# Attention over a long cache: transfers of 64 KiB a partition from one shared memory, 101 units kept between the layers, deviation applied to the products

## The chip, the core and the metric

The kernel runs on one core of one Trainium2 chip. The metric is the device time of one execution in microseconds, lower is better. A core has engines that run side by side: PE multiplies matrices (PEld loads their weights), DVE, ACT and POOL work on vectors, and SP issues the transfers from the chip's memory (HBM). The transfers themselves are carried out by 16 DMA engines, which fetch rows for the 128 partitions of the core's own memory.

## What is computed

Four blocks run one after the other on two tokens: attention, a gated feedforward, and both again with the same weights and the same cache. Each has a layernorm ahead and a residual sum behind it. The cut reference:

```python
def _A_ref(x, k_cache, v_cache, wq, wo):        # x: (2, 1, 512); caches: (2, 8, 32768, 128)
    q = (x @ wq).reshape(B, Sq, 32, 128).transpose(0, 2, 1, 3)
    k = jnp.repeat(k_cache, 4, axis=1)
    v = jnp.repeat(v_cache, 4, axis=1)
    p = _softmax(jnp.einsum("bhqd,bhkd->bhqk", q, k) * 128 ** -0.5, axis=-1)
    o = jnp.einsum("bhqk,bhkd->bhqd", p, v)
    return o.transpose(0, 2, 1, 3).reshape(B, Sq, 4096) @ wo
def _B_ref(x, w_gate, w_up, w_down):            # 512 -> 1792 -> 512
    h = _gelu(x @ w_gate) * (x @ w_up)
    return h @ w_down
for layer in range(2):
    x = x + _A_ref(_layernorm(x), A_k_cache, A_v_cache, A_wq, A_wo)
    x = x + _B_ref(_layernorm(x), B_w_gate, B_w_up, B_w_down)
```

All of it is in float32. K and V together are 512 MiB, read once in each layer. The weights are 8 MiB of wq, 8 MiB of wo, 7 MiB of gate and up (gu) and 3.5 MiB of down (wd), read in each layer too.

## The kernel before

**A layer** takes the 16 pairs of a K/V head and a batch row (`orders`, the second layer in reverse). For each pair `scores` (L226) multiplies the queries with K, `softmax` (L231 to L255) makes the probabilities and turns them, `values` (L269) multiplies them with V, `combine` (L279 to L286) picks the four heads, and after each second pair `project` (L291) multiplies with 1 MiB of wo and adds up in the PSUM tile W. Then `residual` (L296 to L304), `layernorm` (L178 to L192) and `feedforward` (L314 to L337) follow. `layernorm` and `queries` (L203 to L215) open the layer.

**The memory** for what is fetched is 12 slots of 2 MiB (16 KiB in each partition), each of two halves. K and V come in transfers of one whole slot: 128 rows of 16 KiB, 8 of K and 8 of V for a pair. Weights come in halves of 1 MiB with rows of 8 KiB (gu: 7 KiB). The units that this text counts in are 256 KiB: what one matrix multiplication reads (128 partitions x 512 numbers). A slot holds 8 of them.

**The order of transfers** is one list, `stream`. `pump` walks down it and issues each on SP (L92) as soon as a slot or a half is free. `done` gives a slot back and pumps. SP works in order, so the first transfer that has to wait holds back all behind it. Eight completion semaphores are used in turn; a ninth transfer waits until the one eight places ahead of it has landed.

**Between the layers** one slot of K (`KEEPK`) and eight of V (`KEEP`) of the last pair stay where they are, since the second layer begins with that pair. That is 72 units. The three other slots carry the rest of the last pair, then gu, wd and wq, in halves of 1 MiB.

## Time and profile before

| what | value |
|---|---|
| time, median of 3 runs | 2631.04 us (2629.43 to 2633.91) |
| span of the profiled execution | 2629.7 us |
| instructions | 20472 |
| DMA packets of the queue that SP issues on | 80928, 1110.48 MB |
| TensorE clock granted, mean | 0.778 |
| PE busy, DVE busy, ACT busy | 59%, 6%, 2% |

The page gives the span of the profiled execution from its first to its last instruction; the times of the runs are taken around it. A row of the timeline reads: start in us, duration in us, engine, line, operation, what it writes and reads, how many instructions were merged into the row, and in brackets how long the engine had been idle before and what ended that. A product in float32 stands as two MATMUL instructions, so "x8" in a row of 128x512 is four units.

### The profile page before, as it was taken

To read this page: it belongs to the slowest core of one execution; us is meant where nothing else is said; L and a number is where in the kernel's file an instruction comes from. 1 tells how busy PE (TensorE), PEld (TensorE's weight loads), DVE (VectorE), ACT (ScalarE), POOL (GpSimd) and SP (SyncE) were. 2 spreads that over 40 slices of the span, in tenths; PEclk is the share of its full clock that TensorE was granted. 3 is DMA by queue.
4 is the path that set the end of the run, shared out by engine and by line. 5 is a ranking of instruction groups with operands and counts; after the bars stand their busy time and mean duration, and the time that the engine had idled before them with its cause. 6 is when DMAs were issued, how large, how long until landed. Compare 5 with 4: busy or idle time off the path is not lost.

```text
span 2629.7 us, 20472 instructions
## 1 busy us (share of the span) xinstructions
...
## 2 busy tenths in 40 slices
...
DMA  9999999999999999999999999999999999999997
GB/s 411 428 428 427 428 427 428 428 427 427 428 428 427 429 427 428 428 428 428 407 380 415 428 427 429 427 429 427 428 428 428 427 428 428 428 427 428 428 428 332
DMA packets 81303, 1111.99 MB, mean 423 GB/s; under 512 B 9280, under 2 KB 9408, under 8 KB 11712
## 3 DMA queue, kind: packets, MB, share of 16 engines
q1 hardware_dynamic: 80928, 1110.48, 99.5%
...
q14 instruction: 14, 0.11, 0.0%
HBM read 1110.64 MB, written 0.00 MB: 422 GB/s over the span
## 4 chain that ended last, share of the span: by engine, by line
DMA 93%; PE 5%; DVE 1%; issue 0%; ACT 0%; SPq 0%; POOLq 0%; POOL 0%; DVEq 0%; ACTq 0%
DMA slot<-in_vt 49%; DMA slot<-in_kt 42%; PE S L226 2%; PE A L269 1%; DMA slot<-in_wq 1%; PE S L314 1%; PE W L337 0%; DVE mx L231 0%; DMA slot<-in_gu 0%; PE T L248 0%; ACT big L245 0%; PE small L203 0%; DMA xT<-in_x 0%; PE small L282 0%; PE W L291 0%
## 5 line engine op out<-in xcount | busy, mean ns | idle before, releaser
L226 PE MATMUL S<-slot,qpad 128*32 128x512 f32 x4096 | 674.8, 793 | 474.3 <-DMA slot<-in_kt 472.8
L269 PE MATMUL A<-slot,pT 128*16 128x512 f32 x4096 | 683.1, 809 | 429.9 <-DMA slot<-in_vt 429.9
L226 PEld LDWEIGHTS S<-slot,qpad 128*32 128x32 f32 x4096 | 132.4, 129 | 994.2 <-DMA slot<-in_kt 644.2
L269 PEld LDWEIGHTS A<-slot,pT 128*16 128x16 f32 x4096 | 117.0, 113 | 948.3 <-DMA slot<-in_vt 552.6
L231 DVE TENSOR_REDUCE mx<-S 128x1 f32<-128x512 f32 x64 | 44.2, 691 | 1141.3 <-PE S L226 1141.3
L248 PE MATMUL T<-cst,big 128*128 128x128 f32 x256 | 61.1, 384 | 68.4 <-ACT big L245 40.4
L279 DVE TENSOR_SCALAR big<-A,linv 128x512 f32<-128x512 f32 x32 | 24.0, 751 | 1090.0 <-PE A L269 1090.0
L245 ACT ACTIVATE big<-S,bias 128x512 f32<-128x512 f32 x64 | 43.4, 683 | 2449.5 <-DVE bias L241 2449.5
L248 PEld LDWEIGHTS T<-cst,big 128*128 128x128 f32 x256 | 39.2, 190 | 84.4 <-ACT big L245 65.7
L249 DVE COPY pT<-T 128x512 f32<-128x512 f32 x64 | 44.2, 691 | 97.8 <-PE T L248 97.8
L282 PE MATMUL small<-cst,big 128*128 128x128 f32 x128 | 26.1, 337 | 29.9 <-DVE big L279 29.9
L238 PE MATMUL small<-cst,nm 128*128 128x128 f32 x32 | 11.3, 354 | 34.3 <-DVE nm L236 34.3
L203 PE MATMUL small<-slot,xpad 128*32 128x512 f32 x128 | 22.4, 822 | 13.7 <-DMA slot<-in_wq 10.7
L282 PEld LDWEIGHTS small<-cst,big 128*128 128x128 f32 x128 | 16.7, 167 | 78.0 <-DVE big L279 78.0
L291 PE MATMUL W<-slot,oT 128*2 128x512 f32 x128 | 23.4, 814 | 5.1 <-DVE oT L286 5.1
L314 PE MATMUL S<-slot,xpad 128*32 128x256 f32 x224 | 19.6, 483 | 5.2 <-DVE xpad L192 2.9
L251 PEld LDWEIGHTS small<-ls,cst 128*128 128x128 f32 x64 | 17.3, 331 | 0.0
L238 PEld LDWEIGHTS small<-cst,nm 128*128 128x128 f32 x32 | 4.6, 144 | 76.5 <-DVE nm L236 70.8
L251 PE MATMUL small<-ls,cst 128*128 128x2 f32 x64 | 13.5, 280 | 0.0
L245 ACT ACTIVATION_READ_ACCUMULATOR big<-S,bias 128x1 f32 x64 | 12.5, 196 | 0.0
L337 PE MATMUL W<-slot,pT 128*2 128x512 f32 x56 | 11.1, 897 | 1.0 <-DVE pT L331 1.0
L314 PEld LDWEIGHTS S<-slot,xpad 128*32 128x32 f32 x224 | 9.4, 135 | 14.6 <-issue 5.8
...
## 6 DMA issues: line engine op xcount, KB each, us to landing
slot<-in_kt SPq DMA_DIRECT2D x255, 2048.0 KB, 39.1
slot<-in_vt SPq DMA_DIRECT2D x246, 2048.0 KB, 39.1
...
```

What stands on the lines that cost most here:

```text
L203: nc.tensor.matmul(qp[32 * t:32 * t + 32, :], window(k, v), w[:, t, :], start=(k == 0 and v == 0), stop=(k == KC - 1 and v == 1))
L226: nc.tensor.matmul(S[32 * t:32 * t + 32, u, :], qpad[:, g, b, 28 - 4 * c:60 - 4 * c], w[:, 4 * cc + t, :], start=(c == 0), stop=(c == 7))
L231: nc.vector.tensor_reduce(mx[:, u:u + 1], S[:, u, :], axis=AX.X, op=OP.max)
L245: nc.scalar.activation(p[u], S[:, u, :], AF.Exp, bias=bias, scale=SCALE, accum_out=ls[:, u:u + 1])
L248: nc.tensor.transpose(T[:, u, k * P:(k + 1) * P], p[u][:, k * P:(k + 1) * P], ident)
L249: nc.vector.tensor_copy(pT[:, u].rearrange("p k r -> p (k r)"), T[:, u, :])
L251: nc.tensor.matmul(m[:, :2], same, ls, start=True, stop=True)
L269: nc.tensor.matmul(A[32 * t:32 * t + 16, :], pT[:, u, k, 32 * t + 16 * e:32 * t + 16 * e + 16], we[:, t, :], start=(n == 0 and e == 0), st ...
L279: nc.vector.tensor_scalar(md, A, linv, None, op0=OP.mult)
L282: nc.tensor.transpose(m[:, c * P:(c + 1) * P], md[:, c * P:(c + 1) * P], ident)
L291: nc.tensor.matmul(W[32 * t:32 * t + NB, :], oT[:, t, :], w[:, t, :], start=first, stop=final)
L314: nc.tensor.matmul(S[32 * t:32 * t + 32, which, :FN], window(k, v), w[:, r, :], start=(k == 0 and v == 0), stop=(k == KC - 1 and r + 4 >= FR))
```

## The change

K and V are fetched in transfers of 8 MiB, 128 rows of 64 KiB each, 32 units. All of the slots become one tile M of 110 units: three slots A, B and C of 32 units that are used in turn, and three places of four units (`PL`; the last two units of the third are also the buffers of the probabilities). Every transfer has its place in M written down in `plan`. A pair now has 4 transfers of K and V, and the first wq comes in two of 4 MiB.

Between the layers 101 units of the last pair stay: all 64 of V in A and B, the second half of K (32) in C, and five units of the first half of K, which ACT and DVE copy into five PSUM banks. The weights and what is missing of K pass through the three places in transfers of 1 MiB. The second layer first multiplies the kept half of K, four units after each four of wq, and the pieces of the other half of K take the units that come free.

The layernorm is taken apart. `center` subtracts the mean with matrix products; `deviation` works out the reciprocal deviation while the next products already run, and the products are multiplied by it (`scaled`, and the first instructions of the gelu). In `feedforward` gate and up of one block lie side by side, and the 28 units are worked through in two parts of 16 and 12, each followed by its own gelu. `combine` picks the heads with products too, and divides afterwards. In the second layer the last chunk of V comes in pieces of 24, 4 and 4 units (as in the first), gu in four and wd in five transfers into the slots, and the last four units of wd are used as weights of the products, so that the sum comes out turned.

```diff
-NT = 8
-COLS = 4096
-HALF = COLS // 2
+SEQ = 32768
+U = 512
+CH = 32
...
-SLOTS = 12
-KEEP = 8
-KEEPK = 1
+NU = 110
+SLOT_A, SLOT_B, SLOT_C, ZONE = 0, 32, 64, 96
+PL = [96, 100, 104]
+U_P0, U_P1, U_PT = 106, 107, 108
+NPS = 5
+KFREE = CH - NPS
...
-    slots = [cp.tile([P, COLS], F32, name=f"slot{i}") for i in range(SLOTS)]
-    free = [(i, h) for i in range(SLOTS) for h in range(2)]
...
+    M = cp.tile([P, NU * U], F32, name="M")
...
+    def mem(u, n=1):
+        return M[:, u * U:(u + n) * U]
...
     def pump():
-        while stream:
-            key, src, shape = stream[0]
-            n = int(np.prod(shape[1:]))
-            spot = take(n > HALF)
-            if spot is None:
+        while plan:
+            key, src, u, n = plan[0]
+            if any(busy[u:u + n]):
                 return
-            stream.popleft()
-            i, h = spot[0]
-            at[key] = spot, slots[i][:shape[0], h * HALF:h * HALF + n]
-            nc.sync.dma_start(at[key][1], src)
+            plan.popleft()
+            for i in range(u, u + n):
+                busy[i] = True
+            live[key] = u
+            nc.sync.dma_start(mem(u, n), src)
...
+    def free(u, n=1):
+        for i in range(u, u + n):
+            assert busy[i], i
+            busy[i] = False
         pump()
...
+    def chunk(name, l, g, b, h, base, cuts=(CH,), turn=0):
+        src = (kt if name == "k" else vt)[b, g, h]
+        lo = 0
+        where = {}
+        for n in cuts:
+            u = base + (lo + turn) % CH
+            add((name, l, g, b, h, lo), cols(src, lo, n), u, n)
+            for i in range(n):
+                where[lo + i] = ((name, l, g, b, h, lo), u + i)
+            lo += n
+        pieces[(name, l, g, b, h)] = where
...
+        if l == 0:
+            stream("wq", 0, wq, 32, (16, 16), (SLOT_A, SLOT_A + 16))
+            ring = [SLOT_B, SLOT_C, SLOT_A]
+            todo = [(g, b, nm_, h) for g, b in orders[0] for nm_ in "kv" for h in range(2)]
+        else:
+            ring = [SLOT_A, SLOT_B, SLOT_C]
+            g, b = orders[1][0]
+            add(("wq7",), cols(wq, 28, 4), PL[1], 4)
+            stream("wq", 1, wq, 28, (4,) * 7, [PL[0], PL[2], PL[1], PL[0], PL[2], PL[1], PL[0]])
+            where = {}
+            lo = 0
+            for n, u in [(4, PL[2])] + [(4, SLOT_C + 4 * i) for i in range(5)] + [(KFREE - 24, PL[0])]:
+                key = ("k", 1, g, b, 0, lo)
+                add(key, cols(kt[b, g, 0], lo, n), u, n)
+                for i in range(n):
+                    where[lo + i] = (key, u + i)
+                lo += n
+            pieces[("k", 1, g, b, 0)] = where
+            g, b = orders[1][1]
+            chunk("k", 1, g, b, 0, SLOT_C, (12, 20), 20)
+            chunk("k", 1, g, b, 1, SLOT_A, (16, 16))
+            chunk("v", 1, g, b, 0, SLOT_B)
+            add(("wo", 1, g), wo[g], wo_place(g), 4)
+            chunk("v", 1, g, b, 1, SLOT_C)
+            todo = [(g, b, nm_, h) for g, b in orders[1][2:] for nm_ in "kv" for h in range(2)]
+        for i, (g, b, nm_, h) in enumerate(todo):
+            last = i == len(todo) - 1
+            second = (g, b) == orders[l][orders[l].index((g, b))] and orders[l].index((g, b)) % 2 == 1
+            if nm_ == "v" and h == 1 and second and not (last and l == 0):
+                add(("wo", l, g), wo[g], wo_place(g), 4)
+            chunk(nm_, l, g, b, h, ring[i % 3], (24, 4, 4) if last else (CH,))
+            if last and l == 0:
+                add(("wo", l, g), wo[g], wo_place(g), 4)
+        if l == 0:
+            stream("gu", 0, gu, 28, (4,) * 7, [PL[0], PL[2], PL[1], PL[0], PL[2], PL[1], PL[0]])
+            stream("wd", 0, wd, 14, (4, 4, 4, 2), [PL[2], PL[1], PL[0], PL[2]])
+        else:
+            stream("gu", 1, gu, 28, (8, 8, 8, 4), [SLOT_C + 8 * i for i in range(4)])
+            stream("wd", 1, wd, 14, (8, 2, 2, 1, 1), [SLOT_A, SLOT_A + 8, SLOT_A + 10, SLOT_A + 12, SLOT_A + 13])
...
+    def halves(dst, src):
+        nc.scalar.copy(dst[:, :U // 2], src[:, :U // 2])
+        nc.vector.tensor_copy(dst[:, U // 2:], src[:, U // 2:])
+    def center():
+        ws = mem(U_PT + 1)
+        nc.scalar.activation(ws[:, :U // 2], W[:, :U // 2], AF.Copy, accum_out=rs[:, 0:1])
+        nc.vector.tensor_tensor_reduce(ws[:, U // 2:], W[:, U // 2:], zero, 1.0, 0.0, OP.add, OP.add, rs[:, 1:2])
+        for c in (2, 3, 0, 1):
+            nc.tensor.matmul(X[:, c * 4:(c + 1) * 4], ws[:, c * P:(c + 1) * P], two, start=(c == 2), stop=False)
+        for j in range(2):
+            nc.tensor.matmul(X[:, :KC * 4], rs[:, j:j + 1].to_broadcast([P, P]), neg, start=False, stop=(j == 1))
+        xc = X[:, :KC * 4].rearrange("p (c w b) -> p c w b", w=2, b=NB)
+        nc.vector.tensor_copy(xw[:, :, XO:XO + NB], xc[:, :, 1, :])
+        nc.scalar.copy(xin, xc[:, :, 0, :])
+        for b in range(NB):
+            xb = xw[:, :, XO + b]
+            nc.vector.tensor_tensor_reduce(junk, xb, xb, 1.0, 0.0, OP.mult, OP.add, sq2[:, b:b + 1])
+    def deviation(B):
+        v = B[:, 32:32 + NB]
+        nc.tensor.matmul(v, ones.to_broadcast([P, P]), sq2, start=True, stop=True)
+        nc.vector.tensor_tensor_reduce(junk[:, :NB], v, par, 1.0, EPS, OP.mult, OP.add, var)
         nc.gpsimd.tensor_tensor(rstd, var, half, op=OP.pow)
...
+    def scaled(dst, src):
+        nc.scalar.activation(dst[:, :U // 2], src[:, :U // 2], AF.Copy, scale=rstd)
+        nc.vector.tensor_scalar(dst[:, U // 2:], src[:, U // 2:], rstd, None, op0=OP.mult)
...
+    def combine(acc, oT, b):
+        md = mem(U_PT)
+        halves(md, acc)
+        for c in (2, 3, 0, 1):
+            nc.tensor.matmul(X[:, :REP], md[:, c * P:(c + 1) * P], sel[:, 4 * c:4 * c + 4],
+                             start=(c == 2), stop=(c == 1))
+        nc.vector.tensor_tensor(oT[:, :, b], X[:, :REP], linv, op=OP.mult)
...
+        center()
+        s = 0
+        G = [bank[5], bank[7]]
+        g, u, a, th = [mem(U_PT + j // 2)[:, (j % 2) * FN:(j % 2 + 1) * FN] for j in range(4)]
+        for v in range(2):
+            nt = 4 if v == 0 else 3
+            for k in range(KC):
+                for t in range(nt):
+                    key, un = where[s]
+                    at(key)
+                    nc.tensor.matmul(G[v][32 * t:32 * t + 32, :], xw[:, k, XO:XO + 32], mem(un),
+                                     start=(k == 0), stop=(k == KC - 1))
+                    if cut[key] == s:
+                        for q in range(28):
+                            if where[q][0] == key:
+                                free(where[q][1])
+                    s += 1
+                if v == 0 and k == 0:
+                    deviation(X)
...
+            nc.scalar.activation(a[:R], gp, AF.Square, scale=r)
+            nc.vector.tensor_scalar(g[:R], gp, r, None, op0=OP.mult)
+            nc.scalar.activation(u[:R], up, AF.Copy, scale=r)
+            nc.vector.tensor_scalar(a[:R], a[:R], 0.044715, 1.0, op0=OP.mult, op1=OP.add)
+            nc.vector.tensor_tensor(a[:R], a[:R], g[:R], op=OP.mult)
+            nc.vector.tensor_tensor(u[:R], u[:R], g[:R], op=OP.mult)
+            nc.scalar.activation(a[:R], a[:R], AF.Tanh, scale=math.sqrt(2.0 / math.pi))
+            nc.vector.tensor_scalar(a[:R], a[:R], 0.5, 0.5, op0=OP.mult, op1=OP.add)
+            nc.vector.tensor_tensor(th[:R], a[:R], u[:R], op=OP.mult)
+            for j in range(2):
+                nc.tensor.matmul(G[v][:, j * 8:(j + 1) * 8], th[:, j * P:(j + 1) * P], selt, start=True, stop=True)
...
+        tail = 4 if l == 1 else 0
+        for n in range(FD - tail):
+            key, un = where[n]
+            at(key)
+            r, j = divmod(n, 2)
+            v, t = divmod(r, 4)
+            nc.tensor.matmul(W[32 * (n % 4):32 * (n % 4) + NB, :], hT[:, v, j, 2 * t:2 * t + NB], mem(un),
+                             start=(0 < n < 4), stop=(n + 4 >= FD - tail))
+            free(un)
+        if tail:
+            ws = mem(U_PT + 1)
+            halves(ws, W)
+            for c in (2, 3, 0, 1):
+                nc.tensor.matmul(X[:, c * NB:(c + 1) * NB], ws[:, c * P:(c + 1) * P], sel[:, :NB],
+                                 start=(c == 2), stop=False)
+            for n in range(FD - tail, FD):
+                key, un = where[n]
+                at(key)
+                r, j = divmod(n, 2)
+                v, t = divmod(r, 4)
+                for c in range(KC):
+                    nc.tensor.matmul(X[:, c * NB:(c + 1) * NB], mem(un)[:, c * P:(c + 1) * P],
+                                     hT[:, v, j, 2 * t:2 * t + NB], start=False,
+                                     stop=(n == FD - 1 and c == KC - 1))
+            y = sm[:, 0:8]
+            nc.vector.tensor_copy(y, X[:, :KC * NB])
+            nc.sync.dma_start(out, y)
...
+        if (g, b) == last:
+            k0 = pieces[("k", 0, g, b, 0)]
+            free(k0[0][1], KFREE)
+            for i in range(KFREE, KFREE + 3):
+                (nc.scalar.copy if i % 2 else nc.vector.tensor_copy)(bank[psum[i]], mem(k0[i][1]))
+                free(k0[i][1])
+            def hold(h):
+                i = KFREE + 3 + h
+                nc.scalar.copy(bank[psum[i]], mem(k0[i][1]))
+                free(k0[i][1])
+                if h == 1:
+                    free(PL[2], 4)
+            softmax(S, hold)
...
+    center()
+    g, b = last
+    u = at(("wq7",))
+    Q7 = bank[5]
+    for k in range(KC):
+        query_unit(Q7, 7, k, u + k, True, True)
+    free(u, 4)
+    deviation(X)
...
+    for gg in range(7):
         for k in range(KC):
+            key, u = where[4 * gg + k]
+            at(key)
+            query_unit(X, gg, k, u, gg == 0, gg == 6)
+        free(where[4 * gg][1], 4)
+        n = 4 if gg < 6 else CH - i
+        for j in range(n):
+            score_unit(S1, w, i, k1[i][1], i < 4, i >= CH - 4)
+            free(k1[i][1])
...
+    where = pieces[("k", 1, g, b, 0)]
+    held = {30: PL[1], 31: PL[1] + 1, 27: PL[1] + 2, 28: PL[1] + 3, 29: PL[0] + 3}
+    seq = list(range(24)) + [30, 31, 27, 28, 29] + [24, 25, 26]
...
+    values(1, g, b, A1, [pieces[("v", 0, g, b, h)] for h in range(2)], False, 16)
+    combine(A1, oTs[1], b)
...
-        "kt": f(kc.reshape(NB, HKV, NT, COLS, P).transpose(0, 1, 2, 4, 3)),
-        "vt": f(vc.reshape(NB, HKV, 2, 2, 2, 2, 4, 4, P, P).transpose(0, 1, 2, 7, 8, 3, 6, 4, 5, 9)
-                ).reshape(NB, HKV, NT, P, COLS),
+        "kt": f(kc.reshape(NB, HKV, 2, SEQ // 2, P).transpose(0, 1, 2, 4, 3)),
+        "vt": f(vc.reshape(NB, HKV, 2, 2, 4, 4, 4, P, P).transpose(0, 1, 2, 7, 6, 3, 5, 4, 8)
+                ).reshape(NB, HKV, 2, P, CH * U),
```

SP's order shows the sizes. This is the start of the second pair of a layer in the kernel before, which issues K and V of the pair into slots of 2 MiB (4096 numbers a row); the names are tile and tensor:

```order
L92 DMA slot_74<-in_kt 128x4096
L92 DMA slot_75<-in_kt 128x4096
L92 DMA slot_76<-in_kt 128x4096
L92 DMA slot_77<-in_kt 128x4096
L92 DMA slot_66<-in_kt 128x4096
```

In the changed kernel the same place on SP reads as follows; the waits are those written into the instruction, on completion semaphores of transfers (DMAHW) and on PE:

```order
L110 DMA M<-in_kt 128x16384 [waits DMAHW5_49,DMAHW0_49,PE_49]
L110 DMA M<-in_kt 128x16384 [waits DMAHW6_49,PE_49]
L110 DMA M<-in_vt 128x16384 [waits DMAHW7_49,DMAHW2_49,PE_49]
L110 DMA M<-in_wo 128x2048
L110 DMA M<-in_vt 128x16384 [waits DMAHW0_49,PE_49]
```

One row now stands for what were four, and each waits for PE's last reading of its slot. The next place is the end of the first layer. Before, SP issues there the last half of V, then gu, wd and wq:

```order
L92 DMA slot_68<-in_wo 128x2048 [waits DMAHW0_49,PE_49]
L92 DMA slot_68<-in_vt 128x2048 [waits DMAHW1_49,PE_49]
L92 DMA slot_70<-in_vt 128x2048 [waits DMAHW2_49,PE_49]
L92 DMA slot_70<-in_gu 128x1792 [waits DMAHW3_49,PE_49]
L92 DMA slot_71<-in_gu 128x1792 [waits DMAHW4_49,PE_49]
L92 DMA slot_71<-in_gu 128x1792 [waits DMAHW5_49,PE_49]
```

Now the same place on SP is:

```order
L110 DMA M<-in_vt 128x12288 [waits DMAHW7_49,PE_49]
L110 DMA M<-in_vt 128x2048 [waits PE_49,Activation_49]
L110 DMA M<-in_vt 128x2048 [waits Activation_49]
L110 DMA M<-in_wo 128x2048
L110 DMA M<-in_gu 128x2048
L110 DMA M<-in_gu 128x2048 [waits PE_49]
L110 DMA M<-in_gu 128x2048 [waits DMAHW5_49,DMAHW0_49,PE_49]
```

wo has moved behind V, two transfers of gu follow it into free places, and the third of gu waits for PE's reading of wo. The last place is PE's feedforward in the second layer. Before (the name S is the PSUM tile of gate and up, small and W are PSUM, pT is the turned gelu):

```order
L314 MATMUL S<-slot_70,xpad 32x256 [waits DMAHW6_49]
L314 MATMUL S<-slot_70,xpad 32x256 x6
L330 MATMUL small<-cst,big 128x128 [waits DVE_49,PE_49]
L330 MATMUL small<-cst,big 128x128
L337 MATMUL W<-slot_70,pT 2x512 [waits DMAHW7_49,DVE_49]
L337 MATMUL W<-slot_70,pT 2x512 x3
```

And in the changed kernel (bank_79 and bank_81 are the PSUM banks of the two parts, bank_80 is W):

```order
L367 MATMUL bank_79<-M,xw 32x512 x7
L391 MATMUL bank_79<-cst,M 128x8 [waits DVE_49,Activation_49]
L391 MATMUL bank_79<-cst,M 128x8
L367 MATMUL bank_81<-M,xw 32x512 [waits DMAHW2_49]
L367 MATMUL bank_81<-M,xw 32x512 x7
L367 MATMUL bank_81<-M,xw 32x512 [waits DMAHW3_49]
L367 MATMUL bank_81<-M,xw 32x512 x3
L391 MATMUL bank_81<-cst,M 128x8 [waits DVE_49,Activation_49,Pool_49]
L391 MATMUL bank_81<-cst,M 128x8
L401 MATMUL bank_80<-M,hT 2x512 [waits DMAHW4_49]
```

The products of the first gelu (L391) stand on PE between the two parts of gu, so PE waits there for ACT and DVE a first time before it can go on with the second part, and a second time behind it.

501 lines of the change are left out of this document (247 added, 254 removed).

## Prediction

> **What bounds the kernel now.** The page comes first: the span, the DMA slices, the chain, and how long one transfer takes to land.
>
> ```profile
> span 2629.7 us, 20472 instructions
> DMA  9999999999999999999999999999999999999997
> GB/s 411 428 428 427 428 427 428 428 427 427 428 428 427 429 427 428 428 428 428 407 380 415 428 427 429 427 429 427 428 428 428 427 428 428 428 427 428 428 428 332
> q1 hardware_dynamic: 80928, 1110.48, 99.5%
> DMA 93%; PE 5%; DVE 1%; issue 0%; ACT 0%; SPq 0%; POOLq 0%; POOL 0%; DVEq 0%; ACTq 0%
> slot<-in_kt SPq DMA_DIRECT2D x255, 2048.0 KB, 39.1
> slot<-in_vt SPq DMA_DIRECT2D x246, 2048.0 KB, 39.1
> ```
>
> The transfers set the time: 93% of the chain is DMA, and the rate is flat at 428 GB/s outside three places (start, slices 20 to 22, end). So three things can change it: fewer bytes, a higher flat rate, and the places where the queue runs dry. At 428 GB/s a transfer of 2 MiB takes 2.097/0.428 = 4.90 us; eight in flight need 39.1 us to land, 4.89 each.
>
> A transfer with rows half as long has its own row. At the start PE waits for each 1 MiB of wq (8 KiB rows):
>
> ```profile
> 16.33 1.06 PE L203 MATMUL small<-slot,xpad 128*32 128x512 f32 x8 [1.42 <-DMA slot<-in_wq]
> ...
> 23.79 1.94 PE L203 MATMUL small<-slot,xpad 128*32 128x512 f32 x8 [1.42 <-DMA slot<-in_wq]
> ```
>
> Three periods lie between: 7.46/3 = 2.487 us for 1 MiB. Two of them take 4.974, against 4.89 to 4.90 for the same bytes in one transfer. So there is a fixed part of 0.074 to 0.084 us in each transfer, whatever its bytes; I take **0.08**. It may belong to the transfer or to its 8 rows for each DMA engine; both counts are the same here.
>
> **The change, part by part.**
>
> *Bytes.* 72 units are kept now and 101 then: 29 units, 7.25 MiB, 3.63 transfers of 2 MiB at 4.90 us: **-17.8 us**.
>
> *Fixed parts.* The issues count 561 now (255 of K, 246 + 4 of V, 16 each of wq, wo and gu, 8 of wd), and 183 in the changed program (137 of K and V, 10 of wq, 16 of wo, 11 of gu, 9 of wd). 378 fewer at 0.08 us: **-30.2 us** (bounds: 0, if a row of 64 KiB is cut up on its way; 378 x 0.084 = 31.8). An 8 MiB transfer then takes 4 x 4.895 - 3 x 0.08 = 19.34 us, or 434 GB/s. I take nearly the upper end, since the fixed part is seen between two sizes of this very kernel.
>
> The Trainium skill, "DMA: Bandwidth & Descriptors", Rules for kernel authors, holds 1 MiB a transfer for enough; by it the term would be 0. The rows already differ: 2.487 against 2.45 us per MiB above 1 MiB.
>
> *Cover for the large transfers.* PE may give a slot back only after a whole chunk of 32 units. How fast PE works stands here:
>
> ```profile
> 1400.69 16.43 PE L269 MATMUL A<-slot,pT 128*16 128x512 f32 x128
> 2586.59 3.48 PE L269 MATMUL A<-slot,pT 128*16 128x512 f32 x16 [2.98 <-DMA slot<-in_vt]
> 2591.56 1.05 PE L269 MATMUL A<-slot,pT 128*16 128x512 f32 x8 [1.49 <-DMA slot<-in_vt]
> 2594.04 1.91 PE L269 MATMUL A<-slot,pT 128*16 128x512 f32 x8 [1.43 <-DMA slot<-in_vt]
> ```
>
> 64 units take 16.43 us; 8 units after a wait 3.48, so PE is slow first. A chunk is then 3.5 + 24 x 0.23 = 9.0 us. Behind it two more slots are being filled, 38.7 us. The cover holds three times over: 0 us.
>
> *Between the layers.* The five-microsecond windows of before, where the queue falls short (last column GB/s; the one before, the DMA share):
>
> ```profile
> 1305.00:1310.00 5.00, 3.75 (x20) 0.82 (x12) 0.97 (x2) 0.00 (x0) 0.00 (x0) 0.50 0.73 305
> 1310.00:1315.00 5.00, 1.54 (x12) 1.02 (x8) 1.93 (x9) 0.00 (x0) 0.69 (x1) 0.84 0.76 297
> 1315.00:1320.00 5.00, 4.82 (x44) 2.26 (x47) 0.13 (x1) 0.00 (x0) 0.00 (x0) 0.50 0.43 125
> 1320.00:1325.00 5.00, 4.00 (x62) 2.00 (x54) 0.00 (x0) 0.00 (x0) 0.00 (x0) 0.96 0.98 325
> 1355.00:1360.00 5.00, 3.35 (x19) 0.62 (x12) 0.94 (x3) 0.00 (x0) 0.00 (x0) 0.70 0.77 270
> 1360.00:1365.00 5.00, 3.64 (x32) 0.94 (x32) 0.04 (x1) 0.00 (x0) 0.00 (x0) 1.00 0.92 380
> 1400.00:1405.00 5.00, 5.00 (x29) 1.58 (x31) 0.92 (x3) 0.00 (x0) 0.00 (x0) 0.50 0.82 351
> 1405.00:1410.00 5.00, 5.00 (x48) 1.18 (x44) 0.00 (x0) 0.00 (x0) 0.00 (x0) 0.92 0.96 341
> ```
>
> What is missing to 428, times 5 us, over 428, adds up to 12.0 us lost. For the changed kernel I walk along the list, from the landing of the last piece of V, with steps from the feedforward at the end of the program, which runs the same code:
>
> ```profile
> 2596.07 0.75 DVE L279 TENSOR_SCALAR big<-A,linv 128x512 f32<-128x512 f32 x1 [33.89 <-PE A L269]
> ...
> 2600.34 0.69 DVE L296 COPY big<-W 128x512 f32<-128x512 f32 x1 [2.08 <-PE W L291]
> ...
> 2602.29 0.30 PEld L178 LDWEIGHTS small<-xn,avg 128*128 128x128 f32 x2 [0.79 <-PE small L299]
> ...
> 2605.29 9.75 PE L314 MATMUL S<-slot,xpad 128*32 128x256 f32 x112 [1.50 <-DVE xpad L192]
> ...
> 2615.10 0.38 ACT L319 ACTIVATE big<-S 128x256 f32<-128x256 f32 x1 [56.37 <-PE S L314]
> ...
> 2619.08 6.19 PE L337 MATMUL W<-slot,pT 128*2 128x512 f32 x28 [0.52 <-DVE pT L331]
> ...
> 2625.33 0.69 DVE L296 COPY big<-W 128x512 f32<-128x512 f32 x1 [6.30 <-PE W L337]
> ...
> 2627.19 0.35 SPq L358 DMA_DIRECT2D out<-xn  x1
> ```
>
> Behind V three transfers lie in the queue (wo and two of gu): 7.5 us. The 24-unit piece lands 5.0 us ahead of the last, and 32 units take 9.0, so PE ends at 4.0. Combine and project take 4.3 (2596.07 to 2600.34), which frees wo's place at 8.3; data flow about 1.3 later, as these rows show, in which PE ends with wq at 1358.2 and the DMA share is back behind 1359:
>
> ```profile
> 1356.42 1.82 PE L203 MATMUL small<-slot,xpad 128*32 128x512 f32 x8 [0.55 <-DMA slot<-in_wq]
> ...
> 1358.00:1359.00 1.00, 0.24 (x4) 0.00 (x0) 0.68 (x1) 0.00 (x0) 0.00 (x0) 1.00 0.04 16
> 1359.00:1360.00 1.00, 0.66 (x4) 0.42 (x4) 0.25 (x3) 0.00 (x0) 0.00 (x0) 1.00 1.31 279
> ```
>
> Gap 9.6 - 7.5 = 2.1. The next place comes free after centering (4.95 now from 2600.34 to 2605.29, some 1.5 less without the variance) and four units of gu: about 12.8, data at 14.1, while the one transfer in between ends at 12.1: gap 2.0. From there the three places hold 7.5 us of transfers, more than a gelu (2615.10 to 2619.08: 4.0 us), so the two gelus are covered. Behind wd the second centering gives one more gap of about 2, the turn from the queries to K another. The sum is 8 us against 12: **-4 us** (bounds -8, if the gaps close, to +8, if each gap is twice as long).
>
> *The end.* From the last V (2594.04) to the program's last transfer (2627.19) stand 33.2 us. The 42 units of gu and wd need 25.7 us of it, so PE's chain is what ends last, and I go through it: V ends at +4.0 instead of +2.0; combine and project alike; centering -1.5; gu 9.75 alike; one more gelu on PE's path, +4.0; then 8.1 us from wd to the end (2619.08 to 2627.19) become 10 units (4.4 at the slow rate of the 3.48 row), two half copies (1.0), 20 products with weights of 128x128 in two passes, 0.15 us a pass in the row at 2602.29, twice that when PE is slow (6.0 to 12.0; I take 6.5) and a copy, 12.2: +4.1. Sum +8.6; as parts may overlap I take **+7 us** (bounds 0 to +13). Where the cover of the transfers is longer than thought, this is less.
>
> *Start, copies to PSUM, softmax.* They lie beside 19.3 us of transfer each: 0.
>
> The sum: -17.8 - 30.2 - 4 + 7 = -45. On the profiled execution 2629.7 - 45 = 2584.7; the median lies 1.3 above that span, so **2586 us**.
>
> **The rivals.**
>
> *A, rows are cut up.* The change doesn't do what it says to the rate: a row of 64 KiB travels as four of 16, so the fixed part stays. Then only the 10 fewer transfers of weights count, 0.8 us of the 30.2: 2586 + 29 = 2615. For it: 80928 packets are 562 x 144, with the transfer of the result: one packet for each of 128 rows and 16 more, and no row over 16 KiB is seen. The packet count of after decides.
>
> *B, three places are too few.* 22 transfers pass through them, some 7 rounds. If a round costs 4 us more (a gelu uncovered each time): 2614. Against it: 7.5 us of transfer against 4.0 of gelu.
>
> *C, slower.* The engines walk down rows that begin 64 KiB apart instead of 16, and if such starts collide in the memory the flat rate falls. It decides from 45/124.8 = 0.36 us more for each of the 124.8 times 8 MiB, 19.70 us or 426 GB/s; at the lowest rate that the rows show for a full queue, the 2.487 us of wq (421.6 GB/s, 19.90 us), it is 0.56 x 124.8 = +70: 2656. Against it: transfers of 1 MiB show the same period with rows next to each other (wo and the first half of V, 2586.59 to 2591.56: 4.97 for two) and with rows 16 KiB apart (wq, 2.487).
>
> The Trainium skill, "DMA: Bandwidth & Descriptors", Latency and other measured facts, has rates that fall where rows lie a large power of two apart: 207 of 214 GB/s at 512 KiB, half at 4 MiB. By that 3% the time would be an estimated 2586 + 124.8 x 19.34 x 0.034 = 2668; no run here shows 64 KiB.
>
> **How the numbers follow.** My forecast 0.67 (2571 to 2601, from the bounds of the gaps and the end); A 0.13; B 0.07; C 0.11; no change at all 0.02. Within 0.2% (5 us), about what a measurement of this kernel can tell from no change, lies only the last. Faster 0.87, same 0.02, slower 0.11. The range takes in A and B and leaves out C: 2571 to 2622.
>
> **What would show it.** Right: packets of the queue near 184 x 144 = 26,500; flat slices at 433 or 434; landings of K and V 19.3 us apart; three or four gaps of 2 us behind the first layer; some 40 us from the last V to the end, with two gelus. A has 80,000 packets or slices at 428. B has a dip deeper than 380 in the middle slices. C has slices under 426. Wrong would also be a PE that makes SP wait for a slot in mid-layer.

## The result, and the profile after

| kernel | median us (lowest to highest, runs) | to the kernel before, 95% interval |
|---|---|---|
| before | 2630.99 (2629.43 to 2633.91, 4) | 1 |
| changed | 2604.99 (2602.04 to 2608.30, 4) | 0.9907 (0.9892 to 0.9922) |

Faster by 26.0 us; the forecast was 45 us faster, 2586. The time is inside the stated range (2571 to 2622), but 4 us above the part of it that belongs to the forecast's own mechanism (2571 to 2601): it is inside because the range takes in the rivals A and B. Of all the forecasts B's 2614 lies nearest. The profiled execution of the changed kernel is the fastest of its four runs (2602.04 us, span 2599.9).

The page of the changed kernel, the lines that answer to those of before:

```profile
span 2599.9 us, 20241 instructions
GB/s 421 434 433 434 432 434 429 433 435 434 430 433 431 429 435 435 431 433 434 367 352 440 431 433 430 434 434 433 434 431 431 432 430 434 434 433 434 431 428 272
q1 hardware_dynamic: 26496, 1102.86, 98.5%
DMA 58%; PE 28%; another core or an unknown queue 12%; DVE 1%; issue 1%; ACT 1%; SPq 0%; POOL 0%; ACTq 0%; DVEq 0%; POOLq 0%
```

26,496 packets are exactly 184 x 144: a row of 64 KiB is one packet. The flat slices stand at 429 to 435 instead of 427 to 429. The chain gives PE 28%; a likely reason is that with one transfer per chunk PE starts when 8 MiB have landed and SP waits for PE to give the slot back, so that the chain is followed through PE. That isn't a bound: a chunk takes PE half of the period. TensorE's rows that begin with a landing, in the middle of the first layer (the bracket holds the idle time and what ended it):

```profile
359.68 8.66 PE L286 MATMUL bank<-M,qw 128*32 128x512 f32 x64 [5.59 <-DMA M<-in_kt]
379.05 9.21 PE L286 MATMUL bank<-M,qw 128*32 128x512 f32 x64 [10.72 <-DMA M<-in_kt]
398.50 9.71 PE L330 MATMUL bank<-M 128*16 128x512 f32 x64 [5.91 <-DMA M<-in_vt]
417.85 2.76 PE L330 MATMUL bank<-M 128*16 128x512 f32 x12 [9.63 <-DMA M<-in_vt]
```

They start 19.4 us apart (58.17/3 = 19.39), at a landing each, and the forecast had 19.34. SP does wait for PE in mid-layer, which the prediction names as a sign of being wrong: the waits of SP for PE's reading of V, and the median time of 60 transfers of K from issue to landing, are these.

```profile
SPq L110 <- PE bank L330: 561.5, 62, 12.9
...
M<-in_kt SPq DMA_DIRECT2D x60, 50.4
```

But 50.4 us are two and a half periods, so other transfers lie in the queue meanwhile, and the landings keep their distance: the sign came, and it cost nothing. So the dip between the layers (367 and 352 GB/s) and the one at the end (272) must hold what is missing. The first is the sign that the prediction gave for rival B, a dip deeper than 380.

The window of the changed kernel over the whole stretch behind the first layer, and the five-microsecond windows in it that move least (the clock is the third column from the end, GB/s the last):

```profile
1285.00:1355.00 70.00, 51.39 (x328) 17.86 (x321) 9.59 (x39) 6.87 (x18) 1.41 (x3) 0.80 0.80 307
...
1285.00:1290.00 5.00, 5.00 (x48) 1.18 (x40) 0.00 (x0) 0.00 (x0) 0.00 (x0) 1.00 0.61 247
1290.00:1295.00 5.00, 2.68 (x24) 1.61 (x20) 1.02 (x4) 0.85 (x3) 0.00 (x0) 0.98 0.39 126
1295.00:1300.00 5.00, 4.74 (x24) 2.76 (x27) 0.68 (x7) 0.17 (x1) 0.04 (x1) 0.50 0.47 188
1310.00:1315.00 5.00, 4.08 (x24) 0.90 (x18) 0.35 (x1) 0.47 (x1) 0.00 (x0) 0.82 0.46 149
1335.00:1340.00 5.00, 5.00 (x29) 1.23 (x33) 0.34 (x2) 0.00 (x0) 0.00 (x0) 0.59 0.41 133
```

What is missing to 434 is (434 - 307)/434 of 70 us, 20.5 us; the forecast was 8, and before lost 12. (These transfers of 1 MiB have rows of 8 KiB, which took 2.487 us a MiB in the kernel before, 422 GB/s; against that it is 19.1 us.) How it comes about, in the changed kernel's timeline of all engines (SPq is SP's queue of issues, L110 the line that issues every transfer):

```profile
1293.46 12.05 SPq L110 DMA_DIRECT2D M<-in_gu  x5
...
1295.95 1.01 PE L244 MATMUL bank<-cst,sm 128*128 128x16 f32 x4
...
1297.22 1.94 PE L367 MATMUL bank<-M,xw 128*32 128x512 f32 x8 [0.26 <-DVE xw L246]
...
1304.06 1.06 PE L367 MATMUL bank<-M,xw 128*32 128x512 f32 x8 [1.57 <-DMA M<-in_gu]
...
1305.27 0.47 ACT L381 ACTIVATE M<-bank,sm 128x256 f32<-128x256 f32 x1 [7.91 <-PE bank L367]
...
1309.12 4.96 PE L367 MATMUL bank<-M,xw 128*32 128x512 f32 x24
```

And the view of line 110 between 1290 and 1310 us, how long those five transfers of 1 MiB took from issue to landing:

```profile
DMA to landing us min/median/max: 4.7/4.9/6.5
```

The first two, each issued into an empty queue, needed 4.7 and 4.8 us, of which 2.5 are the transfer. The walk had put 1.3 on it instead of 2.3. And PE gives no place back while it waits for the gelu (1305.27 to 1309.12) or works through centering. So a place is out for 4.7 us or more after it was freed, and the other two hold 5 us of stream at best. The rows of the end, from the landing of the 24-unit piece of the last V:

```profile
2550.92 8.71 PE L330 MATMUL bank<-M 128*16 128x512 f32 x64 [8.34 <-DMA M<-in_vt]
...
2576.58 3.63 PE L367 MATMUL bank<-M,xw 128*32 128x512 f32 x24
...
2584.67 4.43 PE L401 MATMUL bank<-M,hT 128*2 128x512 f32 x17
...
2591.02 6.25 PE L416 MATMUL bank<-hT,M 128*128 128x2 f32 x32
...
2597.54 0.35 SPq L421 DMA_DIRECT2D out<-sm  x1
```

The last V lands about 5.0 us behind the first row (two transfers of 1 MiB at 2.49), at 2555.9; from there to the last transfer stand 41.6 us, 8.4 more than before's 33.2. (The expectations below count to the end of the span, 44.2.)

### The profile page after: what moved, and what is told of

The parts are those of the page before. It is cut to its first block, busy times and chain, and to the rows that moved or that the text cites. A ratio compares the mean times of both kernels' runs of the same rounds, so it can differ in the third digit from the quotient of the medians.

```text
span 2599.9 us, 20241 instructions
## 1 busy us (share of the span) xinstructions
PE 1370.0 (53%) x9456; PEld 409.2 (16%) x9456; DVE 147.2 (6%) x433; ACT 73.1 (3%) x196; POOL 3.2 (0%) x12
## 3 DMA queue, kind: packets, MB, share of 16 engines
q1 hardware_dynamic: 26496, 1102.86, 98.5%
## 4 chain that ended last, share of the span: by engine, by line
DMA 58%; PE 28%; another core or an unknown queue 12%; DVE 1%; issue 1%; ACT 1%; SPq 0%; POOL 0%; ACTq 0%; DVEq 0%; POOLq 0%
DMA M<-in_vt 50%; PE bank L330 16%; PE bank L286 8%; DMA M<-in_kt 6%; DMA cst<-in_consts 1%; PE bank L348 1%; PE bank L341 1%; PE bank L367 1%; PE bank L259 1%; DVE M L235 0%; PE bank L401 0%; ACT M L234 0%; PE bank L416 0%; PE bank L242 0%
## 5 line engine op out<-in xcount | busy, mean ns | idle before, releaser
L286 PE MATMUL bank<-M,qw 128*32 128x512 f32 x4096 | 582.3, 731 | 534.8 <-DMA M<-in_kt 534.8
L330 PE MATMUL bank<-M 128*16 128x512 f32 x4096 | 580.1, 730 | 530.9 <-DMA M<-in_vt 530.9
L286 PEld LDWEIGHTS bank<-M,qw 128*32 128x32 f32 x4096 | 142.2, 131 | 963.7 <-DMA M<-in_kt 575.3
L330 PEld LDWEIGHTS bank<-M 128*16 128x16 f32 x4096 | 137.2, 112 | 947.2 <-issue 947.1
L289 DVE TENSOR_REDUCE sm<-bank 128x1 f32<-128x512 f32 x64 | 44.3, 692 | 1107.1 <-PE bank L286 1107.1
L311 ACT ACTIVATE M<-bank,sm 128x512 f32<-128x512 f32 x64 | 43.4, 682 | 1229.3 <-DVE sm L306 1229.3
L314 PE MATMUL bank<-cst,M 128*128 128x128 f32 x256 | 49.2, 335 | 40.6 <-ACT M L311 40.3
L315 DVE COPY M<-bank 128x512 f32<-128x512 f32 x64 | 43.8, 692 | 60.7 <-PE bank L314 60.7
L234 ACT COPY M<-bank 128x256 f32<-128x256 f32 x33 | 12.3, 372 | 1162.0 <-PE bank L330 1155.2
L314 PEld LDWEIGHTS bank<-cst,M 128*128 128x128 f32 x256 | 34.9, 169 | 51.6 <-ACT M L311 51.6
L341 PEld LDWEIGHTS bank<-cst,M 128*128 128x128 f32 x256 | 31.0, 191 | 59.9 <-DVE M L235 59.9
L259 PE MATMUL bank<-M,xw 128*32 128x512 f32 x128 | 21.2, 777 | 3.7 <-DMA M<-in_wq 3.0
L367 PE MATMUL bank<-M,xw 128*32 128x512 f32 x112 | 20.4, 785 | 2.1 <-DMA M<-in_gu 1.6
L311 ACT ACTIVATION_READ_ACCUMULATOR M<-bank,sm 128x1 f32 x64 | 12.5, 196 | 0.0
```

The costliest lines, as they stand in the source:

```text
L259: nc.tensor.matmul(Q[32 * k:32 * k + 32, :], xw[:, k, XO - 2 * g:XO - 2 * g + 32], mem(u), start=start, stop=stop)
L286: nc.tensor.matmul(S[32 * t:32 * t + 32, :], w[:, 28 - 4 * c:60 - 4 * c], mem(u), start=start, stop=stop)
L289: nc.vector.tensor_reduce(mx[:, h:h + 1], S, axis=AX.X, op=OP.max)
L311: nc.scalar.activation(p[h], S[h], AF.Exp, bias=bias, scale=SCALE, accum_out=ls[:, h:h + 1])
L314: nc.tensor.transpose(S[h][:, k * P:(k + 1) * P], p[h][:, k * P:(k + 1) * P], ident)
L315: nc.vector.tensor_copy(mem(U_PT + h), S[h])
```

## The experiments

All are edits of the changed kernel, but for the last. Lines shift by a few with each edit. The kernel before ran beside each of them (2630.2 to 2631.0 us); the changed kernel was not run again.

| run | median us (lowest to highest) | to before, 95% interval |
|---|---|---|
| cut_2mib | 2636.82 (2634.12 to 2640.13) | 1.0022 (1.0012 to 1.0031) |
| rows_16k | 2638.18 (2633.56 to 2639.40) | 1.0025 (1.0014 to 1.0036) |
| no_tail | 2604.32 (2601.26 to 2606.07) | 0.9898 (0.9883 to 0.9912) |
| gelu_order | 2598.18 (2592.21 to 2599.61) | 0.9871 (0.9853 to 0.9889) |
| v_pieces | 2607.07 (2601.94 to 2607.59) | 0.9905 (0.9889 to 0.9922) |
| four_places | 2603.10 (2602.52 to 2604.53) | 0.9896 (0.9882 to 0.9911) |
| half_places | 2610.10 (2607.52 to 2614.95) | 0.9924 (0.9910 to 0.9939) |
| deviation_first | 2614.57 (2612.89 to 2618.72) | 0.9942 (0.9927 to 0.9956) |
| warm_pe | 2591.26 (2590.19 to 2591.75) | 0.9850 (0.9835 to 0.9865) |
| all_three | 2592.10 (2588.26 to 2595.59) | 0.9850 (0.9834 to 0.9867) |
| all_three_warm | 2584.91 (2584.13 to 2586.24) | 0.9827 (0.9812 to 0.9841) |
| before_warm | 2624.45 (2622.55 to 2626.39) | 0.9979 (0.9970 to 0.9989) |

### The fixed part: transfers or rows

cut_2mib moves K and V in transfers of 2 MiB again, with everything else as changed:

```diff
-    def chunk(name, l, g, b, h, base, cuts=(CH,), turn=0):
+    def chunk(name, l, g, b, h, base, cuts=(8, 8, 8, 8), turn=0):
```

(and the same in the loop that calls it.)

> The changed kernel with every chunk of K and V fetched in four transfers of 8 units (rows of 16 KiB) instead of one of 32; places, order and products as they are. Theory one, a fixed part of 0.08 us for each transfer or its rows: 115 whole chunks more or less, three transfers more each, about 350 x 0.08 = 28 us more, 2633 us, flat slices back at 428 GB/s, packets near 76,000. Theory two, the rate comes from fewer waits of the queue or from the shared memory and not from the size: slices stay at 433 to 434 and the time within 5 us of 2605.

rows_16k keeps the transfers of 8 MiB, but each is made of 512 rows of 16 KiB, from a copy of K and V that is laid out in blocks (kb, vb):

```diff
-            nc.sync.dma_start(mem(u, n), src)
+            dst = mem(u, n)
+            if n == CH:
+                dst = dst.rearrange("p (a c) -> p a c", a=4)
+            nc.sync.dma_start(dst, src)
...
-            add((name, l, g, b, h, lo), cols(src, lo, n), u, n)
+            rows = (kb if name == "k" else vb)[b, g, h].rearrange("a p c -> p a c")
+            add((name, l, g, b, h, lo), rows if n == CH else cols(src, lo, n), u, n)
```

> The changed kernel with transfers of 8 MiB left whole, but each of 512 rows of 16 KiB (a copy of K and V in that layout) instead of 128 rows of 64 KiB. If the fixed part belongs to each row, about 2.4 ns at each of 16 engines for every KiB saved, the flat rate is 428 GB/s and the time 2633 us, as with four transfers. If it belongs to each transfer, the rate stays at 434 and the time within 5 us of 2605. Packets near 68,000 in both.

The slices and the packets, first of cut_2mib, then of rows_16k:

```profile
GB/s 414 429 427 428 427 427 428 427 428 428 428 428 428 427 427 428 427 428 427 352 343 430 427 428 428 428 427 428 428 427 427 428 427 428 427 428 428 427 431 240
q1 hardware_dynamic: 78336, 1102.88, 98.6%
```

```profile
GB/s 414 428 427 428 427 428 428 427 428 428 428 428 427 428 427 427 428 429 428 353 339 430 428 428 427 429 428 427 427 428 429 427 428 426 428 428 428 428 432 243
q1 hardware_dynamic: 72576, 1102.86, 98.6%
```

Both are back at 426 to 429 GB/s, and 31.8 and 33.2 us slower than the changed kernel. rows_16k has its transfers and its bytes, and only more rows: 72,576 - 26,496 = 46,080, or 2,880 for each of 16 DMA engines, so 33.2/2,880 = 11.5 ns a row. That is 120 whole chunks, not the 115 of the expectations. cut_2mib has the same 46,080 rows more and, besides, 360 transfers with 16 packets each; 31.8/2,880 = 11.0 ns a row. It isn't slower than rows_16k, so the fixed part belongs to the row, not to the transfer, and it is the whole of the higher rate. The records of single packets in the traces agree: the median is 2.420 us for 64 KiB in the changed kernel and 0.614 for 16 KiB in rows_16k, so four of these take 0.036 us longer, 12 ns for each row more. The prediction's 0.08 us for 8 rows is 10 ns a row. Why a row costs this is open.

Both runs are also slower than the kernel before, by 6 to 7 us, though they fetch 29 units less: without the longer rows the rest of the change would have lost time.

### The end

no_tail lets the products of wd run as in the first layer, so that the last four need no path of their own:

```diff
-        tail = 4 if l == 1 else 0
+        tail = 0
...
-        if tail:
+        if l == 1:
```

> The changed kernel with all 14 units of wd in the second layer multiplied as in the first layer (2 rows by 512 columns), instead of the last four used as weights of 16 products. Theory one, PE's chain ends last and the 32 passes with weights of 128x128 are on it (6.25 us in the profile): they go, four units of 0.25 to 0.45 us come, so 4.5 to 5.2 us less from the last V to the end, 39.5 instead of 44.2 in the profile, 2600 us. Theory two, the landing of wd sets the end: then the product with 512 columns begins later and the end is the same or 1 us later.

gelu_order puts the products that turn the first gelu behind the second part of gu on PE (`turned(v)` holds the lines L390 to L392):

```diff
-            for j in range(2):
-                nc.tensor.matmul(G[v][:, j * 8:(j + 1) * 8], th[:, j * P:(j + 1) * P], selt, start=True, stop=True)
-            nc.vector.tensor_copy(hT[:, v].rearrange("p j r -> p (j r)"), G[v][:, :16])
+        turned(1)
```

(and `turned(0)` stands behind the products of the second part, ahead of its gelu.)

> The changed kernel with the products that turn the first gelu put behind the second part of gu on PE, in both layers, so that PE does not wait for ACT and DVE between the parts. Theory one, the first gelu lies on PE's path: 3.5 us less from the last V to the end (40.7 instead of 44.2), and between the layers the third gap of the queue (5.75 us between the landings of the last gu and the first wd, where 2.5 would be flat) closes to 3.5 or less, another 2 to 3 us: 2599 us. Theory two, the gaps between the layers come from the time from issue to landing alone (4.8 us for 1 MiB): the end gains 3.5 us, the gap stays, 2601 us.

No_tail's second part of gu, its products of wd and its last issue, then gelu_order's last V, its gu behind the first eight products and its last 32 products, all in the second layer:

```profile
2581.12 5.97 PE L367 MATMUL bank<-M,xw 128*32 128x512 f32 x24
...
2592.76 5.27 PE L401 MATMUL bank<-M,hT 128*2 128x512 f32 x25
...
2600.39 0.35 SPq L421 DMA_DIRECT2D out<-sm  x1
```

```profile
2553.84 8.52 PE L330 MATMUL bank<-M 128*16 128x512 f32 x64 [8.54 <-DMA M<-in_vt]
...
2571.81 7.22 PE L372 MATMUL bank<-M,xw 128*32 128x512 f32 x48
...
2588.25 4.50 PE L421 MATMUL bank<-hT,M 128*128 128x2 f32 x32
```

gelu_order takes 6.8 us off, and its 48 products take 7.22 us with no gelu between. All of it comes at the end: from the row of the last V to the end of the span stand 41.6 us (2553.84 to 2595.4) instead of 49.0 (2550.92 to 2599.9). The stretch between the layers moves 291 GB/s and lacks 23.1 us, not less than the changed kernel's 20.5. So theory two has the gaps right, as far as one profile of each tells, and both had too little for the end: besides the gelu the last 32 products shrank, from 6.25 us at a clock of 0.57 to 4.50 at 0.81. no_tail measures the same as the changed kernel (0.7 us less, inside the scatter). From wd's main group of products to the last issue it needs 7.6 us instead of 12.9, but the 24 products of gu ahead of it take 5.97 us, against 3.63 in the changed kernel's profile. The windows of the two, no_tail's and then the changed kernel's, have the reason in the third column from the end:

```profile
2580.00:2585.00 5.00, 4.80 (x19) 1.89 (x22) 0.23 (x2) 0.00 (x0) 0.31 (x1) 0.50 0.41 164
```

```profile
2550.00:2555.00 5.00, 4.08 (x24) 1.00 (x28) 0.00 (x0) 0.00 (x0) 0.00 (x0) 0.57 1.03 433
...
2575.00:2580.00 5.00, 3.93 (x28) 1.41 (x28) 0.91 (x4) 0.13 (x1) 0.31 (x1) 1.00 0.46 187
```

The clock of the window in which these products begin is 0.50 in the one and 1.00 in the other. No expectation had that. One profile of each is all there is, and the changed kernel's is that of its fastest run, so its other runs may have had the slow clock there too.

v_pieces lands the last V of each layer in smaller pieces, so that PE is done with it sooner:

```diff
-            chunk(nm_, l, g, b, h, ring[i % 3], (24, 4, 4) if last else (CH,))
+            chunk(nm_, l, g, b, h, ring[i % 3], (8, 8, 8, 4, 4) if last else (CH,))
```

> The changed kernel with the last chunk of V of each layer in pieces of 8, 8, 8, 4 and 4 units instead of 24, 4 and 4. Theory: PE ends V 3.7 to 3.9 us after the last landing because 24 units reach it at once; with pieces it ends 2 us or less after it. That takes 2 us from the end (42 from the last V to the end instead of 44.2) and 1.9 us from the first gap between the layers (4.37 us between landings to 2.5): 2601 us. Rival: between the layers the gap moves to a later place, and only the end gains: 2603 us.

The windows behind the last V of the first layer in v_pieces, then its second part of gu in the second layer:

```profile
1285.00:1290.00 5.00, 2.56 (x19) 1.50 (x15) 0.42 (x1) 0.37 (x1) 0.00 (x0) 0.87 0.61 254
1290.00:1295.00 5.00, 3.68 (x18) 1.81 (x17) 0.59 (x3) 0.47 (x2) 0.00 (x0) 0.50 0.51 174
```

```profile
2577.49 6.02 PE L367 MATMUL bank<-M,xw 128*32 128x512 f32 x24
```

It gained nothing: 2607.07 us, 2.1 more than the changed kernel and inside the scatter, where 2601 or 2603 was expected. PE has less to do behind the last landing, 2.56 us of 5 instead of 5.00, and the clock of the next window is 0.50, where the changed kernel had 0.98. At the end the 24 products of gu take 6.02 us against 3.63. So in this profile the slower products take back what the pieces bring; warm_pe below tests that cause, not this edit.

### The places between the layers

four_places adds a fourth place of four units, and fetches four units of V again that the changed kernel kept:

```diff
-PL = [96, 100, 104]
+PL = [96, 100, 104, 60]
...
+            add(("v1c",), cols(vt[b, g, 1], CH - 4, 4), PL[3], 4)
...
-            stream("gu", 0, gu, 28, (4,) * 7, [PL[0], PL[2], PL[1], PL[0], PL[2], PL[1], PL[0]])
-            stream("wd", 0, wd, 14, (4, 4, 4, 2), [PL[2], PL[1], PL[0], PL[2]])
+            stream("gu", 0, gu, 28, (4,) * 7, [PL[i] for i in (0, 2, 3, 1, 0, 2, 3)])
+            stream("wd", 0, wd, 14, (4, 4, 4, 2), [PL[i] for i in (1, 0, 2, 3)])
```

(and the places of wq likewise.)

> The changed kernel with a fourth place of four units for what passes between the layers: four units of V are not kept but fetched again, 97 instead of 101 kept. Theory one, the queue runs dry between the layers because a place's round (4.8 us from issue to landing, then PE, then the next issue) is longer than the transfers in the two other places, 5 us: with a fourth place 7.5 us lie in the queue, and the 16 us of gaps fall to 8 or less, for 2.5 us of bytes: 2599 us. Theory two, the gaps come from the chain of the engines (centering, gelu, queries), which no place can shorten: the gaps stay near 16 us and the time rises by 2.5 to 2607 us.

half_places leaves the three places and moves gu, wd and wq through them in transfers of two units:

```diff
-            stream("gu", 0, gu, 28, (4,) * 7, [PL[0], PL[2], PL[1], PL[0], PL[2], PL[1], PL[0]])
+            stream("gu", 0, gu, 28, (2,) * 14, [PL[i] + j for i in (0, 2, 1, 0, 2, 1, 0) for j in (0, 2)])
```

(and the same for wd and wq.)

> The changed kernel with gu, wd and wq between the layers in transfers of two units, 512 KiB, through the same three places, each freed in halves. Theory one (long rounds): a half comes free 0.4 to 0.9 us earlier and lands 1.2 us earlier, so each of some nine gaps shortens by 1 to 2 us, for 17 more transfers with rows of 4 KiB (0.08 us each, 1.4 us): 2597 us. Theory two (the chain of the engines): no change within 3 us of 2605.

The window over the whole stretch, which has 307 GB/s in the changed kernel, for no_tail (whose code up to there is the same), four_places and half_places in this order:

```profile
1285.00:1355.00 70.00, 50.39 (x312) 18.38 (x308) 9.59 (x39) 5.92 (x16) 1.41 (x3) 0.78 0.75 282
```

```profile
1285.00:1355.00 70.00, 54.18 (x364) 21.05 (x356) 10.97 (x43) 6.86 (x18) 1.41 (x3) 0.83 0.83 319
```

```profile
1285.00:1355.00 70.00, 54.65 (x320) 19.45 (x316) 9.68 (x39) 6.02 (x16) 1.41 (x3) 0.79 0.79 286
```

To 434 GB/s these lack 24.5, 18.5 and 23.9 us of 70, and the changed kernel 20.5. Equal code differs by 4 us. By these profiles the fourth place is worth 2 to 6 us, and its four units cost 2.5 to fetch: a small gain at best, and 1.9 us was measured, within the scatter. The window gives the same sign where the rest is alike: 291 GB/s in gelu_order, 316 in the run all_three further down, 4.1 us less lost. Smaller transfers through the same places bring no gain: 2610.10 us, 5.1 more than the changed kernel, where 2597 or 2605 was expected. From the row of the last V to the end of the span that profile has 55.6 us (2554.28 to 2609.9) instead of 49.0, in code that this edit leaves as it was, so the 5.1 us say little about the places.

### The deviation

deviation_first multiplies it into the input ahead of the products, as the kernel before does (`deviation` then stands right behind `center`, and the scalings of the products go):

```diff
-        nc.vector.tensor_tensor_reduce(junk[:, :NB], v, par, 1.0, EPS, OP.mult, OP.add, var)
-        nc.gpsimd.tensor_tensor(rstd, var, half, op=OP.pow)
+        nc.vector.tensor_scalar_add(var2, v, EPS)
+        nc.gpsimd.tensor_tensor(rstd2, var2, half2, op=OP.pow)
+        xb = xw[:, :, XO:XO + NB]
+        nc.vector.tensor_tensor(xb, xb, rstd2.unsqueeze(1).to_broadcast([P, KC, NB]), op=OP.mult)
```

> The changed kernel with the reciprocal deviation worked out and multiplied into the input of the products before they begin, as in the kernel before, instead of applied to the products. Theory: the product, the two DVE steps and the power on POOL that now lie beside the first units of gu (2568.4 to 2569.9 in the profile, 2 us with the hand-overs) come onto the path at the end (+2 us, 46 from the last V) and between the layers (+2 us before gu, +0.5 before the queries, whose copy waits for the deviation already): 2609 us. Rival: the queue hides the two between the layers, and only the end loses: 2607 us.

PE's rows at the first gu, its second part of gu in the second layer and the window over the stretch, in deviation_first:

```profile
1296.33 1.01 PE L247 MATMUL bank<-cst,sm 128*128 128x16 f32 x4
1298.11 0.56 PE L257 MATMUL bank<-sm 128*128 128x2 f32 x2 [0.77 <-DVE sm L253]
1299.96 5.33 PE L373 MATMUL bank<-M,xw 128*32 128x512 f32 x24 [1.30 <-DVE xw L261]
...
2586.44 6.36 PE L373 MATMUL bank<-M,xw 128*32 128x512 f32 x24
```

```profile
1285.00:1355.00 70.00, 48.73 (x292) 18.35 (x284) 8.45 (x37) 4.39 (x14) 1.69 (x3) 0.73 0.71 268
```

9.6 us slower than the changed kernel, where 4 or 2 more was expected. gu begins 3.6 us behind the start of the row before the variance (1296.33 to 1299.96), where in the changed kernel it is 1.3 (1295.95 to 1297.22); the stretch lacks 26.8 us and runs at a clock of 0.73. So at this centering the change is worth 2.4 us, more than the 1.5 that the forecast gave it. Part of the 9.6 us is something else: the 24 products of gu at the end take 6.36 us against 3.63, at a clock of 0.57 against 1.00. How much of the 9.6 us is the clock isn't separated here.

### The clock

v_pieces and no_tail left one suspect: TensorE's granted clock in the stretches where it waits much. warm_pe fills those waits with small products that nobody reads:

```diff
+    def warm(n, B=X):
+        for _ in range(n):
+            nc.tensor.matmul(B[0:32, 256:384], cst[:, 0:32], ident, start=True, stop=True)
...
+            if h == 1 and keep:
+                warm(18)
+            if h == 1 and l == 1 and (g, b) == orders[1][-1]:
+                warm(30)
```

(and warm(3) behind the copies of center and of the last combine of each layer, warm(12, G[1 - v]) ahead of the products that turn a gelu.)

> The changed kernel with small matmuls that nobody reads, put where TensorE only waits: 18 and 30 ahead of the last chunk of V of each layer, 3 behind the copies of combine and center, 12 behind each half of the gate and up products. Theory 1, the granted clock: in the changed kernel's profile the stretch 2585 to 2600 runs at 0.50 to 0.68 and the one at 1295 to 1300 at 0.50, because TensorE had idled 3 to 8 us ahead; kept busy it runs at 1.0, the end behind the last V falls from 44.2 to about 36 and the boundary's loss (81.9 us for 105 units that take 65.2) from 17 to about 13, so 2593 to 2597. Theory 2, the places: the boundary and the end are set by transfers and by dependent steps on VectorE and ScalarE, not by the clock: the end stays at 43 to 45, the boundary at 81 to 85, so 2603 to 2608, or 1 to 3 more where a small matmul is in the way.

all_three joins gelu_order, no_tail and four_places.

> Three edits together: the products that turn the first gelu behind the second half of gate and up, no tail in the down projection, a fourth place of four units. Apart they measured -6.8, -0.7 and -1.9 us against the changed kernel's 2605.0. Theory 1, the clock: the tail's 5 us (13.1 to 8.05 us from the down projection to the output) were lost to a second half of gate and up at the slow clock (5.97 against 3.63 us); with that half at full clock, as the reordered products leave it, they count: 2605.0 - 6.8 - 5 - 1.9, about 2591. Theory 2, a bound behind them that none of them moves: no better than the best of them, 2596 to 2600.

all_three_warm is all_three with the small products, the 12 behind the second gelu alone.

> The three edits together and the small matmuls of the first run of this batch (12 of them behind the second half of gate and up alone). Theory 1, the clock: values of the last V 6.9 instead of 8.5 us and the first matmuls behind it at full clock, about 4 us at the end and 2 to 4 in the boundary below the run without them: 2583 to 2587. Theory 2: within 2 us of the run without them.

In warm_pe, the window over the stretch and one at the last V, then PE at the end:

```profile
1285.00:1355.00 70.00, 55.63 (x414) 24.87 (x406) 10.96 (x43) 6.88 (x18) 1.41 (x3) 0.90 0.86 331
...
2545.00:2550.00 5.00, 3.34 (x33) 0.95 (x36) 0.00 (x0) 0.00 (x0) 0.00 (x0) 1.00 0.98 408
```

```profile
2546.68 7.06 PE L339 MATMUL bank<-M 128*16 128x512 f32 x64 [1.66 <-DMA M<-in_vt]
...
2582.01 4.80 PE L428 MATMUL bank<-hT,M 128*128 128x2 f32 x32
```

In all_three_warm the same stretch:

```profile
1285.00:1355.00 70.00, 56.36 (x410) 23.14 (x406) 10.87 (x43) 6.88 (x18) 1.41 (x3) 0.90 0.92 365
```

More work makes the kernel 13.7 us faster. Between the two profiles 10.4 us lie (2599.9 to 2589.5): 3.9 in the stretch between the layers and 6.2 from the row of the last V on, most of it in the same products taking less time; the rest of the 13.7 is that the changed kernel's profile fell on its fastest run. The clock over the stretch is 0.90 instead of 0.80 and the loss 16.6 instead of 20.5 us; the 64 products of the last V take 7.06 instead of 8.71, the last 32 take 4.80 instead of 6.25. Behind the wait for the last V the clock is 1.00, where the changed kernel had 0.57 (2550 to 2555). The runs lie within 1.6 us, where the changed kernel's lie within 6.3. Theory 1 had 2593 to 2597, 2 us less than the gain that came; theory 2 falls. all_three came 13 us below the changed kernel, as theory 1 had it, and with the small products 7.2 more: 2584.91, in the fastest kernel of this study. Its stretch still lacks 11.1 us.

Last, the kernel before with such products in the same kinds of place:

```diff
+            if (g, b) == orders[l][-1] and n >= NT - 4:
+                warm(5)
...
+        warm(12)
         m = small()
         hT = wk.tile([P, 2, 4, P], F32, name="pT", bufs=1).rearrange("p a b c -> p (a b) c")
```

(and 2, 3 or 5 in the layer norm, combine and residual.)

> The kernel before with such small matmuls in the same kinds of place: 5 ahead of each of the last pieces of V of each layer, 3 behind the copies of combine and residual, 2 and 5 in the layer norm, 12 behind the gate and up products. The question is whether the slow clock is something that the change brought. Theory 1, it is: the kernel before moved V in pieces of 2 MiB, between which TensorE idled 1.4 to 3.0 us instead of 5.6 to 8.3, so it loses little there: 2626 to 2632, and most of the 13.7 us that the small matmuls took from the changed kernel are a cost of the change. Theory 2, both kernels pay it: in the profile of before the stretches 2595 to 2600 and 2605 to 2610 run at 0.50 too; gate and up would take 7.4 instead of 9.75 us, the down projection 3.6 instead of 6.19, the steps ahead of them 2 less, so its end falls from 35.7 to about 29 and its boundary by some 3: 2618 to 2623.

The stretch between the layers, 105 us of it, in before, and in before_warm:

```profile
1305.00:1410.00 105.00, 66.15 (x449) 19.30 (x445) 11.55 (x37) 2.25 (x6) 1.38 (x2) 0.76 0.93 378
```

```profile
1305.00:1410.00 105.00, 71.17 (x567) 25.82 (x566) 11.56 (x37) 2.25 (x6) 1.38 (x2) 0.90 0.97 399
```

Against 428 GB/s before lacks 12.3 us there, before_warm 7.1. The median fell by 5.7 us, less than theory 2 had it and more than theory 1. So both kernels pay for the clock: what these products save is 13.7 us in the changed one and 5.7 in the one before. With them in both, the change is worth 2624.45 - 2591.26 = 33.2 us instead of 26.0.

## Why the prediction was right, and where it was not

The direction, the bytes, the rows and the end came as forecast; the size did not: 26 us instead of 45. That 2605.0 still lies in the stated range is largely luck: only the part added for A and B holds it, A did not happen, and B only in part.

**Bytes and fixed parts** (-17.8 and -30.2): held. Packets, slices and landings are as forecast, rival A (2615) and rival C (2656) are out, and cut_2mib shows what A would have cost: 31.8 us against the 29 put on it. What the text left open, transfer or row, is the row. The rule of the Trainium skill, "DMA: Bandwidth & Descriptors", Rules for kernel authors, by which the prediction put this term at 0, speaks of the size of a transfer. As far as that goes it holds here: with equal rows 2 MiB (2636.8 us) are no slower than 8 MiB (2638.2). Of the length of the rows, which alone makes 33 us here, the rule says nothing. The loss for rows far apart that the same page of the Trainium skill has under Latency and other measured facts, from 512 KiB on, doesn't show at 64 KiB: 434 GB/s.

**Cover for the large transfers** (0): held; the slices in mid-layer don't dip, though SP waits for PE.

**Between the layers** (-4, bounds -8 to +8): this is the step that failed. Lost were 20.5 us, not 8, so the term is +8.5 and 12.5 us off, at its upper bound (with the 19.1 us that allow for the shorter rows, just below it). Two sentences of the walk are wrong. "data flow about 1.3 later": an issue into an empty queue lands 4.7 to 4.8 us later, 2.3 more than the transfer takes. And "the three places hold 7.5 us ..., so the two gelus are covered": that holds only if all three are full when the gelu begins, but behind centering they had just been emptied one by one, and PE waits for gu itself at 1304.06. Rival B, with a chance of 0.07, named this, and its dip came (352 GB/s); its 28 us were too many. That cover is part of it is likely, not shown: the fourth place takes 2 to 6 us of 20.5 by the profiles, but equal code differs by 4, and by the medians its 1.9 us are within the scatter. In all_three_warm, with the clock, 11.1 us are left. The clock is another part (3.9 us in warm_pe), but before paid as much there (5.2), so it does not explain the difference between the two. How the remaining 11.1 us divide between refills and PE's dependent steps stays open; a walk with places enough for all of gu wasn't tried.

**The end** (+7, sum +8.6): 8.4 measured. Its parts came about as listed: 8.7 us of V instead of 9.0, 6.25 for the tail's products instead of 6.5. Taking 7 instead of the sum cost 1.4.

**From the span to the median** (+1.3): was 5.1 here, 2.1 around the span and 3.0 because the profile fell on the fastest of the runs.

Together: 2586 + 12.5 + 1.4 + 3.8 = 2603.7, and 2605.0 was measured; the rest is below the 4 us by which equal code differs.
